# Moving the 32-bit conversion of the last weight from the expert stage to the gate and value products, with the first gate blocks spread out and the last rank product picked by name

## The chip, the cores and the metric

The kernel runs on one core of a Trainium2 chip. A core has TensorE (PE in the profile; its weight loads are PEld), VectorE (DVE), ScalarE (ACT), GpSimd (POOL) and SyncE (SP), which here only issues transfers. Each engine executes its own instructions in order and waits on semaphores for the others. The metric is the device time of one execution in microseconds (us).

## The reference, cut to what matters

Three parts follow one another. The weights of the third part are 64-bit floats in memory.

```
attn   = softmax(q k^T / 8 + bias from cumsum(s), causal) v      # 4 batches, 8 heads, 576 x 64
x      = attn as (2304, 512)                                     # one row for each token
logits = x @ w_gate + modality_bias[modality_id]                 # 8 experts
e      = argmax(logits);  g = softmax(logits)[e]
x      = g * (relu(x @ w1[e]) @ w2[e])                           # expert stage, 512 -> 1024 -> 512
out    = (sigmoid(x @ w_gate2) * (x @ w_val)) @ w_out            # 512 -> 1536 -> 512, float64 weights
```

## The kernel before, in words

**Stages.** Attention takes the 16 pairs of heads in a fixed order of operations (`PERIOD`). The expert stage follows: 9 slots of 256 tokens and 2 half slots of 128, each slot in 8 units, each unit 12 matmuls of the first product (`mm1`, L1004) and 12 of the second product of the unit before (`mm2`, L1024). The units are numbered u = 0 to 71; u = 0 to 15 serve slots 0 and 1 in turn. The gate and value stage (`Moe2.run`) has 36 units of 7 slots, each slot 6 matmuls (L1382) of one product in a fast-multiplication scheme; m = 0 is a gate unit, m = 1 a value unit. The output product ends the kernel (L1537, L1588). Almost every product is made of 3 matmuls over high and low parts, so ScalarE and VectorE split each operand into two.

**The router.** `Router.batch` appends the small operations of one batch to a queue: the logits with the bias as a ninth column (`lg`, copied on GpSimd at L642, summed at L644), maximum, one-hot `oh`, and then `ranks`, which counts with 6 small matmuls how many earlier tokens chose the same expert (`rp`, L656 and L658), then 5 indirect writes into a table on GpSimd's queue (L687). During attention `tick` takes one entry at a time from this queue; for batches 0 to 2 `ranks` waits (`hold`) for a place beside another product. The last batch is left over when attention ends, and `pump` takes entries after each unit u of the expert stage: 9 after u = 0, none after u = 1 and 2, 14 from u = 3 on. When the queue is empty the planning of the slots (`slots`, L782) is queued and pumped likewise; its result is the list of tokens of each slot (`tid`, transposed on TensorE as `itr`, L742, after u = 10).

**The conversion.** `Decode` turns a block of 64-bit floats into 32-bit floats in four tasks of successive steps: `near` on GpSimd (L877), `far` on VectorE (L881), `word` on ScalarE (L885), `tail` on VectorE (L890). SyncE loads the block (`load`, L866), and `tail` issues the next load. The gate and value weights go through it in blocks of 128 x 256, of which the first 8 are converted in the expert stage, one block for every two units from u = 45 on (four tasks each), and 40 in the gate and value stage. The last weight is converted in `last_weight` during the expert stage, in 12 blocks of 128 x 512, one for every two units from u = 17 on, and stored as 32-bit floats in memory (`wo32`); the output stage reads it back.

**The splitting of the gate and value weights.** After its 4 blocks are converted, each set of blocks is summed and split in 7 successive slots (`parts`: `high` on ScalarE L1353, `low` on VectorE L1356, `sub` on VectorE L1359). There are 10 such stretches in the gate and value stage; in 5 of them value units (m = 1) run, in 5 gate units. `snap` (L1391) copies bank X on ScalarE between two products that add to the same bank, so the next X product waits for it.

Of the kernel before, what the change touches and what calls it, by code (L numbers as in the profile page):

```python
# [8 lines left out]
F32 = mybir.dt.float32  # L9
# [491 lines left out]
TROWS, PUMPS = 96, (9, 0, 0, 14)  # L501
# [5 lines left out]
class Router:  # L507
# [92 lines left out]

    def apart(self, group, inst):

        inst = inst.ins
        self.tc.declare_no_dep(inst, group=group, reason="different rows")
        self.tc.add_to_no_dep_group(group, inst)
        self.apart_of[group].append(inst)
# [15 lines left out]
    def batch(self, b, xr, lg):  # L622
# [12 lines left out]
        tb = self.tb.rearrange("p (b t) e -> p b t e", t=5)[:, b]  # L635
# [6 lines left out]
        q.append(lambda: nc.gpsimd.tensor_copy(lg[:, :, :, 8], tb))  # L642
        self.space(4)
        q.append(lambda: V.tensor_reduce(L.unsqueeze(3), lg, axis=AX.X, op=ALU.add))  # L644
        q.append(lambda: V.tensor_reduce(mx.unsqueeze(2), L, axis=AX.X, op=ALU.max))
# [26 lines left out]
        q.append(lambda: V.tensor_tensor(L, L, bc(mx), ALU.subtract))  # L672
        q.append(ranks)
# [83 lines left out]
    def pump(self, n):  # L757
        self.q = [f for f in self.q if f]
        while self.q and n:
            self.q.pop(0)()  # L760
            n -= 1
# [86 lines left out]
class Decode:  # L848
# [7 lines left out]
    def __init__(self, tc, pool, n, srcs, bufs=2):  # L856
        self.nc, self.pool, self.srcs, self.size, self.bufs = tc.nc, pool, srcs, n, bufs
        self.raw, self.n, self.i = {}, 0, 0

    def load(self):  # L860

        if self.n < len(self.srcs):
            src = self.srcs[self.n]
            c, w = src.shape[1:]
            t = self.raw[self.n] = self.pool.tile([128, 8 * self.size], U8, tag="dr", name="dr", bufs=self.bufs)
            self.nc.sync.dma_start(t.rearrange("p (c b) -> p c b", c=c)[:, :, :w], src)  # L866
            self.n += 1

    def stages(self, dst, then=None):

        nc, V, o, i, n = self.nc, self.nc.vector, {}, self.i, self.size
        self.i += 1
        top = lambda: self.raw[i].bitcast(I8).rearrange("p (a b) -> p a b", b=8)[:, :, 4]

        def near():
            o["n"] = self.pool.tile([128, n], I8, tag="dn", name="dn", bufs=2)
            nc.gpsimd.tensor_scalar(o["n"], top(), 56.0, -56.0, ALU.min, ALU.max)  # L877

        def far():
            o["d"] = self.pool.tile([128, n], I8, tag="dd", name="dd", bufs=2)  # L880
            V.scalar_tensor_tensor(out=o["d"], in0=top(), scalar=-72.0, in1=o["n"], op0=ALU.max, op1=ALU.subtract)  # L881

        def word():
            o["t"] = dst()
            nc.scalar.activation(o["t"].bitcast(I32), o["d"], AF.Copy, scale=float(1 << 27))  # L885

        def tail():
            w = self.raw.pop(i).bitcast(I32).rearrange("p (a b) -> p a b", b=2)[:, :, 0]
            t = o["t"].bitcast(I32)
            V.scalar_tensor_tensor(out=t, in0=w, scalar=5, in1=t, op0=ALU.logical_shift_right, op1=ALU.bitwise_or)  # L890
            self.load()
            if then:
                then(o["t"])

        return [near, far, word, tail]
# [362 lines left out]
class Moe2:  # L1258
# [10 lines left out]
    def __init__(self, tc, moe, x2, ids2, wg, wv, wo, out, hd, keep, rp, wo32):  # L1269
# [8 lines left out]
        self.dec = Decode(tc, keep, 256, srcs)  # L1278
# [11 lines left out]
    def last_weight(self, pool):  # L1290

        dec = Decode(self.tc, pool, 512, [self.wo[128 * f : 128 * f + 128, 3:].rearrange("(c p) b -> p c b", c=1) for f in range(12)], 3)
        for _ in range(3):
            dec.load()
        new = lambda: pool.tile([128, 512], F32, tag="dt", name="dt", bufs=2)
        return [dec.stages(new, lambda t, f=f: self.nc.sync.dma_start(self.wo32[128 * f : 128 * f + 128, :], t)) for f in range(12)]
# [365 lines left out]
    def run(self, ctx, rest):  # L1662
# [26 lines left out]
        spread(at(12, 0), at(15, 0), self.rows())  # L1689
        free = 0  # L1690
# [48 lines left out]
        p = []  # L1739
# [24 lines left out]
def kernel(ctx, tc, q, k, v, s, modality_id, moe_w_gate, modality_bias, w1, w2, wg, wv, wo, out):  # L1764
# [10 lines left out]
    with tc.manual_schedule():  # L1775
        ident = cp.tile([128, 128], F32, name="ident")
        make_identity(nc, ident)
        ps_ctx, at_ctx, mo_ctx, ea_ctx, mw_ctx, ex_ctx, xs_ctx, wo_ctx, x1_ctx = (ExitStack() for _ in range(9))
# [44 lines left out]
        def main(u):  # L1823
            if u >= 0:
                router.pump(PUMPS[min(u, 3)])
# [113 lines left out]
```

## Time and profile before

| | |
|---|---|
| median of 3 runs | 933.51 us (931.78 to 933.62) |
| profiled execution, its own time | 931.2 us |
| span of its trace | 929.3 us |
| TensorE busy (matmuls) | 890.6 us, 96% of the span |
| VectorE, ScalarE, GpSimd busy | 687.5, 547.2, 395.8 us |
| mean granted TensorE clock | 0.992 of full speed |

The profiled execution's time is 1.9 us more than the span of its trace. Busy times of different engines overlap, so they do not add up; what bounds a stage has to be read from the stage.

### The profile page before, as it was taken

To read this page: it belongs to the slowest core of one execution; us is meant where nothing else is said; L and a number is where in the kernel's file an instruction comes from. 1 tells how busy PE (TensorE), PEld (TensorE's weight loads), DVE (VectorE), ACT (ScalarE), POOL (GpSimd) and SP (SyncE) were. 2 spreads that over 40 slices of the span, in tenths; PEclk is the share of its full clock that TensorE was granted. 3 is DMA by queue.
4 is the path that set the end of the run, shared out by engine and by line. 5 is a ranking of instruction groups with operands and counts; after the bars stand their busy time and mean duration, and the time that the engine had idled before them with its cause. 6 is when DMAs were issued, how large, how long until landed. Compare 5 with 4: busy or idle time off the path is not lost. (4 is left out here: it accounts for less than half of the span.)

```text
span 929.3 us, 18666 instructions
## 1 busy us (share of the span) xinstructions
PE 890.6 (96%) x6261; PEld 856.7 (92%) x6261; DVE 687.5 (74%) x1549; ACT 547.2 (59%) x1282; POOL 395.8 (43%) x626
## 2 busy tenths in 40 slices
PE   7999999999889998999999999999999999999996
PEld 6898899898789998999998999999999998889996
DVE  5899999999765688867667766767575747868770
ACT  5999899898633656666544545354535345454440
POOL 7988889898822676776620001010000000111111
PEclk8999999999999999999999999999999999999998
DMA  6667659676314458523566422424242308573501
GB/s 170 155 146 177 142 94 141 154 146 225 97 22 80 143 176 262 193 92 92 178 211 215 114 81 80 139 78 136 74 139 68 116 18 300 153 225 110 170 35 45
DMA packets 163866, 125.29 MB, mean 135 GB/s; under 512 B 86737, under 2 KB 147692, under 8 KB 163254
## 3 DMA queue, kind: packets, MB, share of 16 engines
q1 hardware_dynamic: 158566, 112.44, 43.2%
q0 software_dynamic: 3984, 11.32, 4.3%
q8 instruction: 50, 0.82, 0.4%
q14 instruction: 50, 0.41, 0.2%
q10 hardware_dynamic: 1216, 0.30, 0.1%
HBM read 115.95 MB, written 33.23 MB: 161 GB/s over the span
## 5 line engine op out<-in xcount | busy, mean ns | idle before, releaser
L1382 PE MATMUL X<-a,set 128*128 128x384 f32 x864 | 164.1, 337 | 1.9 <-ACT u L1391 0.9
L1382 PEld LDWEIGHTS X<-a,set 128*128 128x128 f32 x864 | 151.7, 188 | 3.8 <-ACT u L1391 1.9
L877 POOL TENSOR_SCALAR dn<-dr 128x256 int8<-128x256 int8 (+1 forms) x60 | 34.4, 573 | 249.0 <-DMA dr<-in_moe_w_val_dram 91.3
L940 POOL TENSOR_TENSOR w<-raw,w 128x512 fp32r<-128x512 f32 x56 | 80.3, 1444 | 45.9 <-ACT w L937 43.6
L1519 POOL DMA_INDIRECT out_dram<-oy,row x18 | 20.2, 1120 | 167.5 <-ACT oy L1543 91.4
L175 POOL TENSOR_SCALAR bias<-cumB,cumT 128x576 f32<-128x576 f32 (+4 forms) x155 | 82.9, 537 | 19.3 <-DVE nm L294 18.3
L1004 PE MATMUL ph<-xT,w 128*128 128x256 f32 x672 | 88.6, 280 | 0.0
L1004 PEld LDWEIGHTS ph<-xT,w 128*128 128x128 f32 x672 | 82.4, 188 | 0.0
L1382 PE MATMUL Y<-a,set 128*128 128x384 f32 x432 | 81.5, 336 | 0.0
L303 ACT ACTIVATE P<-P,nm 128x576 f32<-128x576 f32 (+3 forms) x128 | 79.6, 628 | 0.6 <-DVE nm L294 0.6
L338 DVE TENSOR_TENSOR PL<-pt,PH 128x512 fp32r<-128x512 f32 (+1 forms) x128 | 76.9, 630 | 3.1 <-ACT PH L331 2.6
L1382 PEld LDWEIGHTS Y<-a,set 128*128 128x128 f32 x432 | 76.0, 188 | 0.1
L294 DVE CUSTOM_DVE_ANT_0 P<-sb,bias 128x320 f32<-128x320 f32 (+3 forms) x128 | 67.3, 550 | 6.4 <-PE sb L285 4.8
L1391 ACT COPY u<-X 128x384 f32<-128x384 f32 x72 | 34.5, 480 | 61.1 <-PE X L1382 61.0
L331 ACT CAST PH<-pt 128x512 fp32r<-128x512 f32 (+1 forms) x128 | 64.7, 551 | 5.8 <-PE pt L322 4.7
L322 PE MATMUL pt<-ident,P 128*128 128x128 f32 x448 | 64.1, 277 | 2.8 <-DVE QL L241 1.0
L1008 ACT ACTIVATE hH<-ph 128x256 fp32r<-128x256 f32 x72 | 27.7, 384 | 62.3 <-PE ph L1004 56.4
L940 DVE TENSOR_TENSOR w<-raw,w 128x512 fp32r<-128x512 f32 x56 | 54.7, 976 | 12.1 <-ACT w L937 11.4
L937 ACT CAST w<-raw 128x512 fp32r<-128x512 f32 x112 | 63.6, 619 | 0.0
L285 PE MATMUL sb<-KT,QH 128*128 128x288 f32 (+3 forms) x192 | 56.6, 319 | 4.7 <-DVE nm L294 4.2
L322 PEld LDWEIGHTS pt<-ident,P 128*128 128x128 f32 x448 | 51.6, 142 | 7.8 <-ACT P L303 3.2
L1317 ACT CAST hf<-hp 128x768 fp32r<-128x768 f32 x42 | 34.1, 835 | 38.9 <-DVE hp L1319 35.2
(317 smaller groups left out, 2393.2 us busy)
## 6 DMA issues: line engine op xcount, KB each, us to landing
raw<-in_moe_w_dram SPq DMA_DIRECT2D x80, 512.0 KB
h<-sg SPq DMA_DIRECT2D x72, 192.0 KB
cumB<-cum_d SPq DMA_DIRECT2D x32, 288.0 KB
hp<-h SPq DMA_DIRECT2D x24, 384.0 KB
qraw<-in_q_dram SPq DMA_DIRECT2D x58, 128.0 KB
dr<-in_moe_w_out_dram SPq DMA_DIRECT2D x12, 511.6 KB
dr<-in_moe_w_gate_dram SPq DMA_DIRECT2D x24, 255.2 KB
dr<-in_moe_w_val_dram SPq DMA_DIRECT2D x24, 255.2 KB
```

Of the source, the lines that this page charges most:

```text
L175: (nc.vector if n in FILLB else nc.gpsimd).tensor_scalar(res[i][:rows], cumB[:rows, :m], -1.0, self.cumT[:rows, i, n : n + 1], ALU.mult, A ...
L285: nc.tensor.matmul(self.sb[:rows, o : o + c1 - c0], X[:, T0[i] : T0[i] + rows], h["KT"][:, c0:c1], start=j == 0, stop=j == 1)
L294: nc.vector.tensor_tensor_reduce(out=pt[:rows, :m], in0=self.sb[:rows, o : o + m], in1=self.bias_t[n][i][:rows], op0=ALU.add, op1=ALU.min, ...
L303: nc.scalar.activation(h["P"][i][:rows, : T0[i] + rows], h["P"][i][:rows, : T0[i] + rows], AF.Exp, bias=h["nm", i][:rows], scale=-1.0, acc ...
L322: nc.tensor.transpose(pt[:, c : c + 128], h["P"][i][:, T0[j] : T0[j] + 128], self.ident)
L331: self.nc.scalar.copy(t[:, :z], pt[:, :z])
L338: self.nc.vector.tensor_tensor(t[:, :z], pt[:, :z], h["H"][u][:, :z].bitcast(F32), ALU.subtract)
L937: nc.scalar.copy(v, src)
L940: (eng or nc.vector).tensor_tensor(v, src, h.bitcast(F32), ALU.subtract)
L1004: nc.tensor.matmul(ph, w[:, 128 * dc : 128 * dc + 128], x[:, dc], start=k == 0, stop=k == 11)
L1382: self.nc.tensor.matmul(bank, w[:, c], a[:, h, c], start=first and k == 0, stop=k == 5, skip_group_check=True)
L1391: self.nc.scalar.copy(t, self.o[u, "X"])
```

## The change

The last weight is converted during the gate and value stage, in 24 blocks of 128 x 256 instead of 12 of 128 x 512: block k has its four tasks at slots 31 + 26k/3 (rounded down) to 3 slots later, of 252 slots. The buffers are the space of an activation tile that is free then and of one weight tile. The first 8 gate blocks take one block for every four units from u = 24 on (loads of the first two at u = 23, before at u = 44). The bias copies are made one batch ahead, outside the queue's order of the batch. `pump` takes 14 entries whenever it takes any, but after u = 0 it stops in front of the last batch's `ranks`, so that `ranks` comes after u = 3.

```diff
-TROWS, PUMPS = 96, (9, 0, 0, 14)
+TROWS, PUMP, RANKS = 96, 14, 3
@@ mod_weights
+        for b in range(2):
+            self.bias_in(b)
+
+    def bias_in(self, b):
+        self.nc.gpsimd.tensor_copy(self.lg[b % 2][:, :, :, 8], self.tb.rearrange("p (b t) e -> p b t e", t=5)[:, b])
@@ batch
-        q.append(lambda: nc.gpsimd.tensor_copy(lg[:, :, :, 8], tb))
-        self.space(4)
         q.append(lambda: V.tensor_reduce(L.unsqueeze(3), lg, axis=AX.X, op=ALU.add))
+        if b + 2 < self.B:
+            q.append(lambda: self.bias_in(b + 2))
...
+        if b == self.B - 1:
+            self.last_ranks = ranks
         q.append(ranks)
@@ pump
-    def pump(self, n):
+    def pump(self, u):
         self.q = [f for f in self.q if f]
-        while self.q and n:
+        n = 0 if 0 < u < RANKS else PUMP
+        while self.q and n and (u or self.q[0] is not self.last_ranks):
@@ last_weight
-        dec = Decode(self.tc, pool, 512, [self.wo[128 * f : 128 * f + 128, 3:].rearrange("(c p) b -> p c b", c=1) for f in range(12)], 3)
-        for _ in range(3):
+        raw = [self.ap.tile([128, 3072], U8, tag=f"xs{i}", name=f"dx{i}", bufs=1) for i in range(3)]
+        top = self.rp.tile([128, 4096], U8, tag="raw2_3", name="dx3", bufs=1)
...
+        at = [(128 * f, 256 * l) for f in range(12) for l in range(2)]
+        dec = Decode(self.tc, 256, [
+            self.wo[r : r + 128, 8 * c + 3 : 8 * c + 2048].rearrange("(c p) b -> p c b", c=1) for r, c in at
+        ], room)
+        for _ in range(4):
             dec.load()
@@ Moe2.run
+        def last_weight():
+            for k, stages in enumerate(self.last_weight()):
+                for i, task in enumerate(stages):
+                    put(at(4, 3) + 26 * k // 3 + i, [task])
+
+        put(at(3, 5), [last_weight])
@@ kernel
-        for k, stages in enumerate(glu.last_weight(pool(wo_ctx, "dec", side="right", reuse_waits="tile"))):
-            for i, task in enumerate(stages):
-                put(2 * k + i - 55, [task])
-        put(-28, [wo_ctx.close, open_xs, glu.dec.load, glu.dec.load])
+        put(-49, [open_xs, glu.dec.load, glu.dec.load])
-                put(2 * k + i - 27, [task])
+                put(4 * k + i - 48, [task])
```

## Rows read from the trace of the kernel before

**Rows 1.** By stretch: us; busy (instructions) of PE, PEld, DVE, ACT, POOL; clock; DMA; GB/s.

```profile
309.00:390.00 81.00, 75.57 (x634) 73.85 (x633) 66.64 (x82) 50.61 (x104) 60.32 (x51) 1.00 0.65 211
...
390.00:460.00 70.00, 69.72 (x596) 69.52 (x595) 50.74 (x71) 42.17 (x92) 49.53 (x43) 1.00 0.33 101
...
545.00:757.00 212.00, 212.00 (x1212) 211.77 (x1212) 140.54 (x309) 99.61 (x222) 16.09 (x34) 1.00 0.29 95
```

**Rows 2.** TensorE's waits, by window: total us, times, longest.

```profile
PE rp L656 <- DVE oh L649: 4.5, 1, 4.5
...
PE sb L1024 <- DVE hL L1009: 3.4, 3, 1.5
PE y L1024 <- DVE hL L1009: 1.6, 3, 0.9
```

**Rows 3.** Timeline, end of attention: start, us, engine, line, output, count.

```profile
252.99 1.04 PE L988 MATMUL mtr<-ident,xg 128*128 128x128 f32 x8
...
255.56 1.29 DVE L994 TENSOR_TENSOR xT<-mtr,xT 128x512 fp32r<-128x512 f32 x2 [1.50 <-ACT xT L993]
...
258.50 0.20 PE L656 MATMUL rp<-oh,tri 128*128 128x48 bf16 x1 [4.48 <-DVE oh L649]
258.67 2.86 PE L1004 MATMUL ph<-xT,ew 128*128 128x256 f32 x12
...
263.12 1.60 PE L1004 MATMUL ph<-xT,ew 128*128 128x256 f32 x12
...
266.00 1.60 PE L1004 MATMUL ph<-xT,ew 128*128 128x256 f32 x12
```

**Rows 4.** By stretch, TensorE alone: us, busy (matmuls), granted clock, DMA, GB/s.

```profile
239.00:241.00 2.00, 0.51 (x5) 1.00 0.90 316
...
258.00:260.00 2.00, 1.50 (x12) 0.68 0.00 0
260.00:262.00 2.00, 2.00 (x12) 0.50 0.03 8
```

**Rows 5.** Timeline, from the ranks to the list of tokens.

```profile
268.40 0.19 DVE L677 TENSOR_TENSOR R<-R,oh 128x40 f32<-128x40 f32 x1
...
286.93 0.61 SPq L1047 DMA_DIRECT2D ids<-tid  x2
...
289.13 0.31 PE L742 MATMUL itr<-ident,tid 40*128 40x40 f32 x2
```

**Rows 6.** VectorE's groups, 309 to 391 us: count, busy us, mean ns, idle before.

```profile
L890 DVE SCALAR_TENSOR_TENSOR dt<-dr,dt 128x512 int32<-128x512 int32 x12 | 17.6, 1469 | 0.0
L881 DVE SCALAR_TENSOR_TENSOR dd<-dr,dn 128x512 int8<-128x512 int8 x12 | 15.7, 1311 | 2.6 <-POOL dn L877 2.6
```

**Rows 7.** VectorE's and GpSimd's groups, 545 to 757 us.

```profile
L1412 DVE TENSOR_TENSOR sg<-u,sg 128x384 f32<-128x384 f32 x28 | 15.9, 567 | 1.0
...
L890 DVE SCALAR_TENSOR_TENSOR ds<-dr,ds 128x256 int32<-128x256 int32 x36 | 14.7, 419 | 3.3 <-ACT ds L885 2.9
L881 DVE SCALAR_TENSOR_TENSOR dd<-dr,dn 128x256 int8<-128x256 int8 x36 | 14.1, 422 | 0.3 <-POOL dn L877 0.3
...
L877 POOL TENSOR_SCALAR dn<-dr 128x256 int8<-128x256 int8 x34 | 16.1, 473 | 175.6 <-DMA dr<-in_moe_w_val_dram 80.9 <-DMA dr<-in_moe_w_gate_dram 44.6 <-DVE sg L1403 29.6
```

**Rows 8.** Timeline of ScalarE in two stretches of weight splitting among value units.

```profile
636.47 0.47 ACT L1391 COPY u<-X 128x384 f32<-128x384 f32 x1
...
680.39 0.47 ACT L1391 COPY u<-X 128x384 f32<-128x384 f32 x1
```

**Rows 9.** Chain that ended last: TensorE's pieces behind those copies.

```profile
637.14 2.21 PE X L1382 x12
...
681.26 2.08 PE X L1382 x12
```

**Rows 10.** Timeline, first batch of the router during attention.

```profile
108.30 0.23 DVE L672 TENSOR_TENSOR r_L<-r_L,r_mx 128x40 f32<-128x40 f32 x1
...
112.05 0.19 PE L656 MATMUL ptx<-oh,tri 128*128 128x48 bf16 x1
```

More of the change, by code (lines that the diff above doesn't have):

```diff
@@ L634, in batch @@
         bc = lambda a: a.unsqueeze(2).to_broadcast([128, 5, 8])
-        tb = self.tb.rearrange("p (b t) e -> p b t e", t=5)[:, b]
         L, mx, eq, em = (tile_([128, 5, 8], "L"), tile_([128, 5], "mx"), tile_([128, 5, 8], "eq"), tile_([128, 5], "em"))
@@ L848, with __init__, pool_room @@
 class Decode:
-    def __init__(self, tc, pool, n, srcs, bufs=2):
-        self.nc, self.pool, self.srcs, self.size, self.bufs = tc.nc, pool, srcs, n, bufs
+    def __init__(self, tc, n, srcs, room):
+        self.nc, self.room, self.srcs, self.size = tc.nc, room, srcs, n
         self.raw, self.n, self.i = {}, 0, 0
+    @staticmethod
+    def pool_room(pool, n):
+        shapes = {"dr": ([128, 8 * n], U8), "dn": ([128, n], I8), "dd": ([128, n], I8)}
+        return lambda tag, i: pool.tile(*shapes[tag], tag=tag, name=tag, bufs=2)
     def load(self):
@@ L864, in load @@
             c, w = src.shape[1:]
-            t = self.raw[self.n] = self.pool.tile([128, 8 * self.size], U8, tag="dr", name="dr", bufs=self.bufs)
+            t = self.raw[self.n] = self.room("dr", self.n)
             self.nc.sync.dma_start(t.rearrange("p (c b) -> p c b", c=c)[:, :, :w], src)
@@ L869, in stages @@
     def stages(self, dst, then=None):
-        nc, V, o, i, n = self.nc, self.nc.vector, {}, self.i, self.size
+        nc, V, o, i = self.nc, self.nc.vector, {}, self.i
         self.i += 1
@@ L875, in near @@
         def near():
-            o["n"] = self.pool.tile([128, n], I8, tag="dn", name="dn", bufs=2)
+            o["n"] = self.room("dn", i)
             nc.gpsimd.tensor_scalar(o["n"], top(), 56.0, -56.0, ALU.min, ALU.max)
         def far():
-            o["d"] = self.pool.tile([128, n], I8, tag="dd", name="dd", bufs=2)
+            o["d"] = self.room("dd", i)
             V.scalar_tensor_tensor(out=o["d"], in0=top(), scalar=-72.0, in1=o["n"], op0=ALU.max, op1=ALU.subtract)
@@ L1277, in __init__ @@
         srcs = [cols(w, f, j, l).rearrange("(c p) b -> p c b", p=128) for f in range(self.NF) for w in (wg, wv) for j, l in blocks]
-        self.dec = Decode(tc, keep, 256, srcs)
+        self.dec = Decode(tc, 256, srcs, Decode.pool_room(keep, 256))
         self.wo = wo.bitcast(U8)
@@ L1286, in preload, with last_weight @@
         self.nc.scalar.activation(t, t, AF.Sigmoid)
-    def last_weight(self, pool):
-        dec = Decode(self.tc, pool, 512, [self.wo[128 * f : 128 * f + 128, 3:].rearrange("(c p) b -> p c b", c=1) for f in range(12)], 3)
-        for _ in range(3):
+    def last_weight(self):
+        raw = [self.ap.tile([128, 3072], U8, tag=f"xs{i}", name=f"dx{i}", bufs=1) for i in range(3)]
+        top = self.rp.tile([128, 4096], U8, tag="raw2_3", name="dx3", bufs=1)
+        dr = [raw[0][:, 0:2048], raw[1][:, 0:2048], top[:, 0:2048], top[:, 2048:4096]]
+        cut = lambda a, n, k: raw[2][:, a + n * k : a + n * k + n]
+        places = {
+            "dr": dr, "dn": [cut(0, 256, k).bitcast(I8) for k in range(2)],
+            "dd": [cut(512, 256, k).bitcast(I8) for k in range(2)], "dt": [cut(1024, 1024, k).bitcast(F32) for k in range(2)],
+        }
+        room = lambda tag, i: places[tag][i % len(places[tag])]
+        at = [(128 * f, 256 * l) for f in range(12) for l in range(2)]
[3 more added lines that the diff above has]
+        for _ in range(4):
             dec.load()
-        new = lambda: pool.tile([128, 512], F32, tag="dt", name="dt", bufs=2)
-        return [dec.stages(new, lambda t, f=f: self.nc.sync.dma_start(self.wo32[128 * f : 128 * f + 128, :], t)) for f in range(12)]
+        store = lambda t, r, c: self.nc.sync.dma_start(self.wo32[r : r + 128, c : c + 256], t)
+        return [dec.stages(lambda k=k: room("dt", k), lambda t, r=r, c=c: store(t, r, c)) for k, (r, c) in enumerate(at)]
     def load_x(self, t, raws):
@@ L1777 @@
         make_identity(nc, ident)
-        ps_ctx, at_ctx, mo_ctx, ea_ctx, mw_ctx, ex_ctx, xs_ctx, wo_ctx, x1_ctx = (ExitStack() for _ in range(9))
+        ps_ctx, at_ctx, mo_ctx, ea_ctx, mw_ctx, ex_ctx, xs_ctx, x1_ctx = (ExitStack() for _ in range(8))
         ps = pool(ps_ctx, "psum", space=PSUM)
@@ L1824, in main @@
             if u >= 0:
-                router.pump(PUMPS[min(u, 3)])
+                router.pump(u)
             if not router.q and phase[0] == 0:
```

## Prediction

> **What bounds the kernel now.** I read the busy times by stretch first, then TensorE's waits window by window, then the timeline where a wait stands. The reader is to see that TensorE sets the time almost everywhere, so that only its gaps can be won and only new gaps can cost. In the gate and value stage it is busy for all of 212 us, while VectorE is busy for 140.5 us of them and GpSimd for 16.1 [rows 1]. In the expert stage two stretches differ: from 309 to 390 us, where the last weight is converted, TensorE is busy for 75.57 of 81 us; from 390 to 460 us, where gate blocks are converted instead, for 69.72 of 70 [rows 1]. VectorE's share falls between them from 66.64/81 = 82% to 50.74/70 = 72%. TensorE's waits in the first of them are for `hL`, which VectorE makes: 3.4 + 1.6 = 5.0 us [rows 2]. The other large wait is a single one, 4.5 us for `oh` in front of the last rank product [rows 2], at the end of attention.
>
> **The change part by part.**
>
> *The last rank product.* After the transposes of slot 1 (252.99 + 1.04 = 254.03) TensorE's next instruction is `rp` at 258.50, which waits for the router's chain on VectorE; only then comes the first product of unit 1, at 258.67 [rows 3]. With `rp` after u = 3, that product waits for its own operand `xT` alone: VectorE makes it in two halves, 255.56 to 256.85 [rows 3], so the first half is there at 255.56 + 1.29/2 = 256.2, and the second at 256.85, before the seventh of the 12 matmuls wants it. A unit at full clock takes 266.00 - 263.12 = 2.88 us [rows 3]. Unit 2 would begin at 256.2 + 2.88 = 259.1 instead of 263.12, which is 4.0 us earlier. The six small matmuls still have to run later, 258.67 - 258.50 = 0.17 us, and a little around them, so I take 3.7.
>
> In this sum 1.6 us are clock: behind the wait of 4.48 us the granted clock is 0.68, then 0.50, which is 1.2 GHz, and the unit from 258.67 to 263.12 takes 4.45 us instead of 2.88 [rows 3, 4]. Would the clock fall again behind the gap that is left, 256.2 - 254.03 = 2.2 us? Between 239 and 241 us TensorE is busy for only 0.51 of 2 us and the clock stays at 1.00 [rows 4]. The new gap is nearer to that one than to 4.48, so I take no fall; with a fall the gain is 4.0 - 1.6 - 0.2 = 2.2. The bounds of this term are 2.2 and 4.0.
>
> What is queued behind the moved product: the ranks, the table writes, the list of tokens, its transposes `itr`. Before, the multiplication with the ranks began at 268.40, right behind `hL` of unit 3 [rows 5]. It will now wait until TensorE has ended unit 3's second product (1.44 us, half a unit), the rank product and its addition, about 1 us later against TensorE. The list had arrived by 286.93 and `itr` ran at 289.13 [rows 5], so some 2.2 us of slack are there, and 1.2 stay. If that cover were gone, each microsecond over it would come back on TensorE.
>
> *The bias copies and the four removed empty entries.* Four copies on GpSimd of about 0.27 us move, and the chain of a batch starts some entries earlier. In the first batch that chain ended at 108.30, but its rank product had to wait for its place at 112.05 [rows 10], as it will again: nothing behind the hold moves. I take 0; bounds are 4 x 0.27 = 1.1 us either way, if VectorE's order around them or GpSimd's wait for the sum were felt.
>
> *What leaves the expert stage.* Twelve blocks take VectorE 12 x (1.469 + 1.311) = 33.4 us, half of its 66.64 us in that stretch [rows 1, 6], plus ScalarE, GpSimd and transfers. The gain has two readings. By idle time: 81 - 75.57 = 5.43 us, less what stays at the later stretch's rate, 0.28 x 75/70 = 0.3, gives 5.1. By counts: 634 matmuls in 81 us against 596 in 70; at the later rate they take 634 x 70/596 = 74.5 us, which gives 6.5 [rows 1]. The second also holds what is lost when the matmuls around a stall run further apart, so I lean to it: 6.0. The eight gate blocks come into this stretch at half their old density; at the old one TensorE lost 0.28 us in 70 [rows 1], so they cost nothing. SyncE's queue loses twelve loads and twelve stores among the expert weights, for which TensorE does not wait now; nothing is gained there.
>
> *What comes into the gate and value stage.* One block is 0.473 us on GpSimd, 0.422 + 0.419 us on VectorE and one word on ScalarE [rows 7]: for 24 blocks 24 x 0.841 = 20.2 us of VectorE, which has 212 - 140.5 = 71.5 us free [rows 1]. The same four tasks run there 36 times now without a wait of TensorE. What hides them is slack, and it is thin in one kind of place: the stretches in which weights are split while value units run. There ScalarE's `high` waits for VectorE's `sub`, the snap queues behind it, and the next X product needs the snap. The snap ends at 636.94 and the product starts at 637.14; the next time 680.86 and 681.26 [rows 8, 9]: slack of 0.2 and 0.4 us. By the slots of the new blocks, `tail` falls in front of that `sub` in two of these five stretches and `far` in two others, 0.42 us each; so each may add up to about 0.4 less its slack. In the fifth the block follows it. I take 0.8 us for all five and for the ScalarE-heavy stretches of gate units, with bounds 0 and 5 x 0.84 = 4.2. SyncE waits with each new load and store for the `tail` before it; behind it stand stores of products, read much later, and the loads of gate and value blocks, for which GpSimd already waits [rows 7] while TensorE does not. The stores end at slot 234, the reading back starts at slot 243.
>
> GpSimd's `near` runs among VectorE's work: `sg<-u,sg` took 567 ns on average with 34 of them in the window, little over its sibling forms [rows 7]. The Trainium skill, page "SBUF — State Buffer", section "Who interferes with whom", says that a VectorE instruction with two SBUF inputs and a GpSimd instruction that reads SBUF exclude each other for the whole instruction. By that rule one more 0.473 us would be lost in each of the five tight stretches, 2.4 us, and the stage would cost 3.2 instead of 0.8; the trace so far bears little of it out.
>
> *The sum.* 931.2 - 3.7 - 6.0 + 0.8 = 922.3 us for an execution like the profiled one. The median of the runs is 2.3 us above it, so 924.6 us, a gain of 8.9 us or 1.0%.
>
> **The rivals.** *A: the clock falls all the same, or the first product of unit 1 finds another wait.* Rank gain 2.2 or less: 926.1. For it: the clock's reaction to a gap of 2.2 us is not in the trace, and `hL` of unit 1 comes behind the chain and a weight split on VectorE, about 0.3 us ahead of its use. Against it: rows of 4.
>
> *B: the gate and value stage gives part of it back.* VectorE's lag reaches the snaps in most of the ten stretches, or the exclusion above holds: 3 to 6 us, so 927 to 930. For it: slacks of 0.2 and 0.4 us. Against: 36 blocks without a wait.
>
> *C: the waits of the expert stage stay.* If VectorE and GpSimd are late for the splitting of the expert weights and not for the conversion, the gain there is 0 to 2 us, and the time 929 to 931. Against it: the next stretch has the same splitting, 0.28 us idle.
>
> *D: slower.* VectorE sets the pace of the gate and value stage. If each of its new instructions delays TensorE in full, 20.2 us come in: 933.5 - 9.7 + 20.2 = 944.0. It decides from 9.7/24 = 0.40 us a block on, one of the two instructions. For it: VectorE runs without a gap in the splitting stretches. Against it: 71.5 us free, and between those stretches it waits for TensorE.
>
> **How the numbers follow.** Forecast 0.64, A 0.14, B 0.13, C 0.04, D 0.05. The predicted time is the forecast's, 924.6. Its lower end: gains of 4.0 and 6.5, no cost, 933.5 - 10.5 = 923.0, and 2 us for the spread of the runs (931.78 to 933.62) and the bias term: 921. The upper end takes in A and most of B: 930. About 0.2% of the time, 1.9 us, is what a measurement of this kernel can tell from no change. Faster by more than that needs under 931.6: forecast, A, nearly all of B, half of C, 0.91; within it 0.04; slower 0.05.
>
> **What would show it.** Right: `rp` in the trace after unit 3 without a wait, a gap in front of unit 1's first product of about 2.2 us with the clock at 1.00 behind it; between units 17 and 41 some 8.5 matmuls a us, as from 390 to 460 us [rows 1], with TensorE idle under 0.5 us; in the gate and value stage 2.1 to 2.2 us for 12 matmuls throughout [rows 9]. Wrong: new waits of X products for `u` on ScalarE above 2 us in total, waits for `hL` that stay, `itr` waiting for the list, or a clock of 0.50 after attention.

## The result, and the profile after

The changed kernel takes 920.75 us (median of 5 runs, 920.44 to 922.45) where the kernel before took 933.62 us beside it: a ratio of 0.9866, 95% interval 0.985 to 0.9882, or 12.5 us by the ratio. The forecast was 924.6 us with 921 to 930 around it: faster, as said, and 0.25 us under the lower end. The profiled execution after takes 920.75 us, with a span of 918.5 us (before 929.3), so the spans differ by 10.8 us.

By stretch, as in [rows 1] (us; busy and instructions of PE, PEld, DVE, ACT, POOL; clock; DMA; GB/s), the kernel after:

```profile
309.00:390.00 81.00, 81.00 (x694) 81.00 (x693) 44.54 (x76) 49.13 (x105) 57.62 (x48) 1.00 0.38 121
390.00:460.00 70.00, 70.00 (x598) 70.00 (x597) 37.48 (x60) 40.56 (x85) 45.22 (x36) 1.00 0.39 125
545.00:757.00 212.00, 210.52 (x1200) 209.21 (x1199) 153.83 (x345) 105.21 (x241) 27.22 (x56) 1.00 0.40 132
```

In the first stretch TensorE has no idle time any more, and 694 matmuls stand where 634 stood. In the third it has 1.48 us of it, where there was none.

TensorE's waits from 245 to 500 us and from 545 to 770 us (total us, times, longest), answering [rows 2]:

```profile
PE yh L1135 <- DVE hT L1126: 2.7, 3, 1.3
PE ph L1017 <- ACT xT L1006: 2.4, 1, 2.4
...
PE ph L1017 <- DVE xT L1007: 0.3, 1, 0.3
...
PE X L1407 <- ACT u L1416: 1.5, 3, 0.9
```

The waits for `oh` and for `hL` are gone. The wait for `hT`, at the end of the expert stage, was there before with 3.4 us. New are a wait of the first product of unit 1 for `xT`, and three waits of X products for the copies of ScalarE.

The end of attention, TensorE's timeline (start, us, then engine, line, output, count), as [rows 3]:

```profile
250.64 1.04 PE L1001 MATMUL mtr<-ident,xg 128*128 128x128 f32 x8
254.07 0.39 PE L1017 MATMUL ph<-xT,ew 128*128 128x256 f32 x1 [2.40 <-ACT xT L1006]
254.80 1.58 PE L1017 MATMUL ph<-xT,ew 128*128 128x256 f32 x11 [0.34 <-DVE xT L1007]
257.66 1.60 PE L1017 MATMUL ph<-xT,ew 128*128 128x256 f32 x12
...
263.41 0.20 PE L661 MATMUL rp<-oh,tri 128*128 128x48 bf16 x1
...
263.58 1.68 PE L1017 MATMUL ph<-xT,ew 128*128 128x256 f32 x12
```

The rank product `rp` stands behind unit 3 and waits for nothing. Unit 1 takes 257.66 - 254.07 = 3.59 us, where it took 4.45 us [rows 3]. The granted clock is 1.00 in every 2 us from 252 to 264 us; before it fell to 0.50 [rows 4].

The list of tokens, as [rows 5]:

```profile
264.00 0.20 DVE L684 TENSOR_TENSOR R<-R,oh 128x40 f32<-128x40 f32 x1
...
283.91 0.31 PE L749 MATMUL itr<-ident,tid 40*128 40x40 f32 x2
...
284.13 0.62 SPq L1060 DMA_DIRECT2D ids<-tid  x2
```

In the first batch the router's chain ends 2.7 us earlier than in [rows 10]; its rank product still waits for its place, which comes 0.9 us earlier:

```profile
105.58 0.64 DVE L677 TENSOR_TENSOR r_L<-r_L,r_mx 128x40 f32<-128x40 f32 x1
...
111.16 0.19 PE L661 MATMUL ptx<-oh,tri 128*128 128x48 bf16 x1
```

In the gate and value stage (groups from 545 to 757 us, as [rows 7]: count, busy us, mean ns, idle before), the new blocks are the `dx` rows, close to the prices that the forecast used, and `sg<-u,sg` beside them takes 558 ns (before 567). The 12 large blocks of [rows 6] are gone from the expert stage.

```profile
L1437 DVE TENSOR_TENSOR sg<-u,sg 128x384 f32<-128x384 f32 x27 | 15.1, 558 | 0.9
L894 DVE SCALAR_TENSOR_TENSOR dx<-dx,dx 128x256 int8<-128x256 int8 x23 | 10.0, 436 | 0.0
L903 DVE SCALAR_TENSOR_TENSOR dx<-dx,dx 128x256 int32<-128x256 int32 x23 | 9.6, 418 | 2.0 <-ACT dx L898 2.0
...
L890 POOL TENSOR_SCALAR dx<-dx 128x256 int8<-128x256 int8 x22 | 10.6, 489 | 3.8 <-DVE dx L894 3.8
```

Between the first and the last Z product of this stage there are 260.02 us, 2.46 us more than before. Set beside each other unit by unit, five steps make the loss: 0.3, 1.1, 0.3, 0.3 and 0.7 us, at units 5, 7, 16, 22 and 28, each in a stretch in which weights are split. The largest is seen in the timeline (SPq is SyncE's queue):

```profile
547.36 0.33 SPq L879 DMA_DIRECT2D dx<-in_moe_w_out_dram  x1
547.74 0.42 SPq L1320 DMA_DIRECT2D wo<-dx  x1
548.22 0.42 SPq L1438 DMA_DIRECT2D h<-sg  x1
...
548.75 0.94 SPq L879 DMA_DIRECT2D dr<-in_moe_w_val_dram  x2
...
554.02 0.40 POOL L890 TENSOR_SCALAR dn<-dr 128x256 int8<-128x256 int8 x1 [19.21 <-DMA dr<-in_moe_w_val_dram]
554.46 0.43 DVE L894 SCALAR_TENSOR_TENSOR dd<-dr,dn 128x256 int8<-128x256 int8 x1 [1.75 <-POOL dn L890]
...
558.27 0.47 ACT L1416 COPY u<-X 128x384 f32<-128x384 f32 x1
...
558.79 2.34 PE L1407 MATMUL X<-a,set 128*128 128x384 f32 x12 [0.87 <-ACT u L1416]
```

A load and a store of a new block, both behind that block's `tail`, go out ahead of the loads of two value blocks. Those land for GpSimd's `dn` at 554.02, 5.3 us after their issue; VectorE's `dd` waits for it, the split that follows is late, ScalarE's snap too, and the X product waits 0.87 us.

At two of the other steps, the snap of ScalarE and the chain's piece behind it, as [rows 8, 9]:

```profile
624.80 0.47 ACT L1416 COPY u<-X 128x384 f32<-128x384 f32 x1
...
669.06 0.47 ACT L1416 COPY u<-X 128x384 f32<-128x384 f32 x1
```

```profile
625.33 2.34 PE X L1407 x12
632.87 2.10 PE X L1407 x12
...
669.59 2.35 PE X L1407 x12
```

The snap ends at 625.27, the product starts at 625.33, and such a piece takes 2.34 us where its neighbours take 2.10. The slack there was thinner than [rows 9] make it look: in the chain a piece starts where the one before it ends, and the timeline of the kernel before has the product of 637.14 at 637.00, 0.06 us behind the snap, with its weights already waiting for the snap:

```profile
637.00 2.03 PEld L1382 LDWEIGHTS X<-a,set 128*128 128x128 f32 x12 [0.18 <-ACT u L1391]
637.00 2.34 PE L1382 MATMUL X<-a,set 128*128 128x384 f32 x12
```

The span's 10.8 us lie so, from milestones of both timelines: attention (to `mtr` of slot 1) 2.35; from there to unit 5, 2.87; units 17 to 41, 7.22; units 42 to 70, 0.19; unit 71 to the first Z, 0.47; Z to Z -2.46; the rest 0.16.

### The profile page after: what moved, and what is told of

It is laid out like the page before. It is cut to its first block, busy times and chain, and to the rows that moved or that the text cites. A ratio compares the mean times of both kernels' runs of the same rounds, so it can differ in the third digit from the quotient of the medians.

```text
span 918.5 us, 18756 instructions
## 1 busy us (share of the span) xinstructions
PE 888.4 (97%) x6261; PEld 853.9 (93%) x6261; DVE 667.2 (73%) x1573; ACT 547.2 (60%) x1294; POOL 397.2 (43%) x638
## 5 line engine op out<-in xcount | busy, mean ns | idle before, releaser
L890 POOL TENSOR_SCALAR dn<-dr 128x256 int8<-128x256 int8 x48 | 24.5, 512 | 227.5 <-DMA dr<-in_moe_w_val_dram 95.7
L1022 DVE SCALAR_TENSOR_TENSOR hL<-ph,hH 128x256 fp32r<-128x256 f32 x72 | 30.4, 422 | 49.2 <-ACT hH L1021 47.6
L953 DVE TENSOR_TENSOR w<-raw,w 128x512 fp32r<-128x512 f32 x56 | 46.6, 832 | 19.2 <-ACT w L950 18.0
```

The lines of the kernel that those rows point to most:

```text
L953: (eng or nc.vector).tensor_tensor(v, src, h.bitcast(F32), ALU.subtract)
```

## The experiments

Microseconds gained are by the ratio to the kernel before, run on the same chip beside it, times 930, its median there (929.57, 930.43 and 930.00 us in the three groups of runs).

**The three parts alone.** `e1_rank_only`, the kernel before with

```diff
-        while self.q and n:
+        n = 0 if 0 < u < RANKS else PUMP
+        while self.q and n and (u or self.q[0] is not self.last_ranks):
```

> The kernel before with the last rank product moved behind unit 3 and nothing else; biases and conversion stay as they were. My theory: the move by itself is worth what its place in the trace says, 2.9 to 3.7 us, so about 3.0 us under the kernel before, with the clock at 1.00 where it was 0.50, no wait for oh, and the transposes of slot 1 at the end of attention at their old time, within 0.3 us. Rival: the 2.35 us by which attention itself ended earlier in the changed kernel come from the order of the router's work, which the move touches too; then this kernel ends attention 1 to 2.4 us earlier as well and is 4 to 6 us faster.

927.01 us, ratio 0.9975 (0.9958 to 0.9993): 2.3 us gained. There is no wait for `oh`, the clock stays at 1.00, and attention ends at 252.62 us, within 0.4 us of before. The theory holds, its size within the interval.

`e2_bias_only`, the kernel before with the copies taken out of the batches' chains and the queue's counts shortened by one:

```diff
+        for b in range(2):
+            self.bias_in(b)
...
-        q.append(lambda: nc.gpsimd.tensor_copy(lg[:, :, :, 8], tb))
-        self.space(4)
```

> The kernel before with only the bias copies taken out of the batches' chains and the four empty entries removed; the last rank product stays before unit 1. The prediction gave this part 0 with 1.1 us either way. Theory: this part is what made attention end 2.35 us earlier in the changed kernel, because each batch's chain is shorter by one GpSimd copy and four empty entries; then the transposes of slot 1 come 1.5 to 2.4 us earlier here and the time falls by 1.5 to 2.5 us, while the wait for oh of about 4.5 us and the clock of 0.50 behind it stay. Rival: those 2.35 us are variation from one profiled execution to the next; then attention ends within 0.5 us of the kernel before and the time is within 1 us of it.

929.92 us, ratio 1.0002 (0.9986 to 1.0019). The profiled execution ends attention at 249.68 us, 3.3 us before the first profile of the kernel before, and its time is 927.49 us, yet the median is the same. The theory's place was right in one profile and its time wrong over 12 runs.

`e3_weight_late`, the kernel before with the other half of the change:

```diff
-        for k, stages in enumerate(glu.last_weight(pool(wo_ctx, "dec", side="right", reuse_waits="tile"))):
...
+                    put(at(4, 3) + 26 * k // 3 + i, [task])
...
-                put(2 * k + i - 27, [task])
+                put(4 * k + i - 48, [task])
```

> The kernel before with only the conversion moved: the last weight in 24 blocks during the gate and value stage, the first gate blocks in every fourth unit; biases and the last rank product as before. Theory: units 17 to 41 take about 70.5 us instead of 77.9 and the expert stage gains 7.4 us in all, the gate and value stage gives 2.45 us back, so 4.9 us net, about 928.6 us, with attention and the wait for oh as before. Rival: part of the 7.4 us came from the units starting earlier and at full clock, not from the conversion; then the stage gains under 6 us and the net is under 3.5 us.

925.68 us, ratio 0.9958 (0.9942 to 0.9973): 3.9 us gained. Units 17 to 41 take 72.89 us from first product to first product (before 80.11), and the five steps stand at the same units with 0.33, 1.23, 0.35, 0.27 and 0.68 us, 2.71 us from Z to Z. So they belong to the blocks alone. The stages say 4.9 us, inside the interval.

**The parts in pairs, and both kernels again.** The parts alone add up to 6.0 us (2.3 - 0.2 + 3.9), the changed kernel had 12.5. So the pairs were run: `e9_rank_weight` (the changed kernel with the biases as before), `e10_bias_weight` (with the last rank product before unit 1) and `e11_rank_bias` (with the conversion in the expert stage), and once more the changed kernel (`e7_after_again`) and the kernel before (`e8_before_again`), neither edited. The edit of `e10_bias_weight`:

```diff
-        n = 0 if 0 < u < RANKS else PUMP
-        while self.q and n and (u or self.q[0] is not self.last_ranks):
+        n = (8, 0, 0, 14)[min(u, 3)]
+        while self.q and n:
```

`e9_rank_weight` undoes the edit of `e2_bias_only`, `e11_rank_bias` that of `e3_weight_late`.

> The changed kernel once more, beside the kernel before, on the chip of the next runs. The rank move alone gave 2.3 us and the conversion alone 3.9 us, the biases nothing: 6.2 us where the changed kernel had 12.9 us in its first comparison. Theory: the parts add up, by the stages of the traces 3.1 to 3.7 + 7.5 - 2.4 = 8.2 to 8.8 us, and the rest of the first comparison is a matter of which runs of the kernel before it met, so the gain here is 8 to 9 us and attention's end differs by up to 3 us between profiled executions of the same code. Rival: the parts help one another, and the gain stays at 11.5 us or more.

> The kernel before, profiled a second time. In its first profile unit 5 began 18.77 us after the transposes of slot 1, in the two kernels with the same order there 17.45 us, and the wait for oh was 4.48 us against 3.17 us. Theory: that 1.3 us is a chance of the first profiled execution, as is the time at which attention ends: here 17.4 to 17.5 us and a wait for oh of 3.1 to 3.2 us. Rival: the two other kernels shortened it; then 18.7 us and 4.5 us again. In either case units 17 to 71 take 165.1 to 165.8 us.

> The changed kernel with the bias copies as in the kernel before: rank move and conversion together. The changed kernel gave 10.2 us beside the parts' 2.5, 0 and 3.9. Theory: the stages add up, as in the traces (rank 2.7, conversion and thinner gate blocks 7.1 + 0.5, gate and value stage -2.5), and single comparisons are off by 1 to 2 us; then about 8 us under the kernel before, with unit 5 at 266.0 us as in the other kernels with the later rank product. Rival one: the bias copies give 2 to 3 us as soon as the rank product is out of the way; then only 6.4 us. Rival two: rank move and conversion help one another; then 10 us.

> The changed kernel with the last rank product before unit 1 again. Theory: stages add up, 7.1 + 0.5 - 2.5 = 5.1 us under the kernel before; the wait for oh is 3.17 us, and unit 5 begins at 267.1 to 269.4 us, depending on attention's end and on whether the clock falls behind that wait. Rival: the bias copies count with the conversion; then 7 us or more.

> The changed kernel with the conversion in the expert stage as before, rank move and bias copies together. Theory: 2.7 us under the kernel before, as the rank move alone (2.5 us measured); units 17 to 42 take 79.5 to 80.1 us. Rival: the bias copies give 2 to 3 us once the rank product is out of the way; then 5 us under the kernel before, and unit 5 begins before 265 us.

| part moved | median, us | ratio (95%) | gained, us |
|---|---|---|---|
| rank | 927.01 | 0.9975 (0.9958 to 0.9993) | 2.3 |
| bias | 929.92 | 1.0002 (0.9986 to 1.0019) | -0.2 |
| weight | 925.68 | 0.9958 (0.9942 to 0.9973) | 3.9 |
| rank, weight | 922.05 | 0.9901 (0.9872 to 0.993) | 9.2 |
| bias, weight | 923.68 | 0.9923 (0.9896 to 0.9951) | 7.2 |
| rank, bias | 925.91 | 0.9947 (0.9929 to 0.9965) | 4.9 |
| all three | 920.22 | 0.989 (0.9871 to 0.9908) | 10.2 |

Each part can be read four times, as the difference that it makes with each choice of the others. Weight: 3.9, 9.2 - 2.3 = 6.9, 7.2 + 0.2 = 7.4, 10.2 - 4.9 = 5.3; mean 5.9. Rank: 2.3, 5.3, 5.1, 3.0; mean 3.9. Bias: -0.2, 2.6, 3.3, 1.0; mean 1.7. A single ratio is good for some 2 us either way, so a mean over four such pairs for about 1.4 (worked out as 2 x the root of 8, over 4), and no reading stands out from its mean by more than two ratios can differ. Neither rival with parts that help one another is shown; the kernels with one part alone came out low, all three. Against their expectations: the changed kernel's 10.2 us lie between theory and rival. The two pairs with the bias copies gained what their rivals said (7.2 and 4.9 us, theories 5.1 and 2.7), and unit 5 begins at 264.22 us in the pair of rank and bias, before 265; the pair without the copies gained 9.2, between its theory's 8 and the 10 of its second rival.

What the profiles show of it, with the times from `mtr` of slot 1 to unit 5, and from unit 17 to unit 42:

| profile | end of attention | wait for `oh` | to unit 5 | 17 to 42 |
|---|---|---|---|---|
| before | 252.99 | 4.48 | 18.77 | 80.11 |
| before again | 251.42 | 3.17 | 15.97 | 80.09 |
| bias | 249.68 | 3.16 | 17.46 | 79.54 |
| weight | 251.75 | 3.17 | 17.44 | 72.89 |
| bias, weight | 252.98 | 3.16 | 17.46 | 72.89 |
| rank | 252.62 | none | 13.75 | 79.90 |
| rank, bias | 250.48 | none | 13.74 | 80.30 |
| rank, weight | 256.96 | none | 13.75 | 72.89 |
| after | 250.64 | none | 15.90 | 72.89 |
| after again | 252.58 | none | 13.75 | 72.89 |

The conversion's 6.7 to 7.4 us are as steady as a number can be. The rank product's are 3.7 us (17.45 - 13.75) or 2.2 us (15.97 - 13.75), and the difference is the clock. Behind the same wait of 3.17 us the kernel with only the weight moved fell to half the clock and the second profile of the kernel before did not (2 us each, TensorE alone: busy, matmuls, clock, DMA, GB/s; first the kernel with the weight moved, then the kernel before again):

```profile
254.00:256.00 2.00, 0.05 (x2) 1.00 0.01 0
256.00:258.00 2.00, 2.00 (x18) 0.72 0.00 0
258.00:260.00 2.00, 2.00 (x11) 0.50 0.12 8
```

```profile
254.00:256.00 2.00, 0.37 (x8) 1.00 0.00 0
256.00:258.00 2.00, 2.00 (x18) 1.00 0.12 8
258.00:260.00 2.00, 2.00 (x19) 1.00 0.00 0
```

So my expectation of 17.4 to 17.5 us for the kernel before again was wrong by the clock, and right on the wait. Both first profiles have something that no later one has: ScalarE's `xT` starts 1.95 us (before) and 2.80 us (after) behind the start of `mtr`, in the 12 others 0.64 us. That is the 1.31 us by which the first wait for `oh` was longer, and the 2.16 us by which the first profile after was slower to unit 5. What held ScalarE there is open.

Attention ends on average at 251.7 us in the nine profiles with the copies ahead and at 253.2 us in the five without (256.96 among them), with a scatter of 2 to 3 us in each, so the ends alone don't price the copies. A stretch that repeats does. From the start of the sixth group of `ot` products in attention to that of the twelfth (69.52 to 113.67 us before, 69.38 to 112.78 after), four of the five profiles without take 44.10 to 44.19 us and all nine with them 43.38 to 43.48: 0.75 us. Of this 0.47 us stand at one place (first the kernel before, then after):

```profile
77.23 0.51 PE L361 MATMUL ot<-PH,vhl 128*128 128x512 f32 x1 [1.02 <-DVE QL L259]
```

```profile
76.06 0.41 POOL L605 COPY lg<-tb 128x40 f32<-128x40 f32 x2 [4.79 <-DVE tb L599]
76.66 0.50 PE L361 MATMUL ot<-PH,vhl 128*128 128x512 f32 x1 [0.55 <-DVE QL L259]
```

The copies of the first two batches now stand in GpSimd's order right behind the making of `tb`, the table of biases, and GpSimd is idle until it is there. VectorE's five instructions that make it take 1.30 to 1.31 us in all beside the idle GpSimd, in each of the nine profiles, and 1.75 to 1.77 us beside a busy one in four of the other five. The fifth is the 256.96 (rank and weight moved): there they take 3.62 us, the last of them alone 1.45 beside a GpSimd instruction, where it takes 0.33 in the others.

```profile
75.67 1.40 POOL L203 TENSOR_TENSOR khl<-kraw,khl 128x576 fp32r<-128x576 f32 x1
75.79 1.45 DVE L599 TENSOR_TENSOR tb<-tb,fill 128x160 f32<-128x160 f32 x1
```

TensorE then waits 3.25 us for `QL`, the clock falls behind the wait, and the stretch takes 47.95 us. What the copies give beyond the 0.75 us, within the 1.7 and its 1.4 either way, stays open.

The clock adds to the scatter of the ends. Behind the gap that [rows 4] show, 1.26 to 1.60 us long at 237 to 243 us, it stayed at 1.00 in eight of the 14 profiles and fell in six, which cost some 1.5 us each (2 us each, TensorE alone; first after, then `e12_placed_two`, an experiment below):

```profile
240.00:242.00 2.00, 2.00 (x13) 1.00 0.03 4
```

```profile
240.00:242.00 2.00, 1.94 (x9) 0.59 0.03 4
```

In the profile after, the list's transposes `itr` no longer have slack. In the second profile of the changed kernel they waited:

```profile
284.41 0.31 PE L749 MATMUL itr<-ident,tid 40*128 40x40 f32 x2 [0.64 <-DMA tid<-tab,row]
```

In the kernel with rank and weight moved the wait is 0.77 us, in one other kernel 0.3 us, in the rest none.

**The loss of the gate and value stage.** `e4_no_conversion`, the changed kernel whose new blocks only load and store, so that the conversion itself is left out:

```diff
-        return [dec.stages(lambda k=k: room("dt", k), lambda t, r=r, c=c: store(t, r, c)) for k, (r, c) in enumerate(at)]
+        zero = places["dt"][0]
+        self.nc.vector.memset(zero, 0.0)
+        return [[lambda: None] * 3 + [lambda r=r, c=c: (dec.load(), store(zero, r, c))] for r, c in at]
```

> The changed kernel without the four engine instructions of each of the 24 blocks: their loads and stores stay in their queue, the stores write zeros, so the last product has a zero weight. Theory: of the 2.45 us that the gate and value stage gave back, some 1.1 us at unit 7 come from loads of value blocks that stand behind a load and a store of the new blocks in SyncE's queue. In the changed kernel that queue waits there for VectorE's tail; without the tail it doesn't wait, so that here nearly all 2.45 us come back and the time is about 918.3 us. Rival one: it is the bytes of the new transfers, not the wait, that delay those loads; then the 1.1 us at unit 7 stay and the time is about 919.4 us. Rival two: the stage's loss isn't the blocks' at all; then the time stays at 920.7 us.

919.33 us, ratio 0.9882 (0.9858 to 0.9906). All five steps are gone, that of unit 7 too. The value blocks' loads are issued at 547.20 us instead of 548.75, and `dn` begins 2.9 us behind them instead of 5.3:

```profile
544.30 0.42 SPq L879 DMA_DIRECT2D dx<-in_moe_w_out_dram  x1
544.77 0.44 SPq L1320 DMA_DIRECT2D wo<-dx  x1
...
547.20 1.38 SPq L879 DMA_DIRECT2D dr<-in_moe_w_val_dram  x2
...
550.12 0.58 POOL L890 TENSOR_SCALAR dn<-dr 128x256 int8<-128x256 int8 x1 [19.47 <-DMA dr<-in_moe_w_val_dram]
```

The same bytes pass here, so it is not the bytes (rival one) but when they pass: behind a `tail` that VectorE is late with, and just ahead of loads that are needed. The first of those loads also needs its own block's `tail`, which VectorE starts at 547.68 us after and at 546.72 here: 0.96 of the 1.55 us are VectorE's, the rest is the queue's. The median alone is what rival one gave, 919.4, and over the theory's 918.3; it is the steps in the trace that decide between them. From Z to Z 1.05 us remain, spread over the units without a wait behind 545 us; the kernel with the bias part alone, which has no new block there, shows 0.78 us of the same drift. What makes it is open.

`e5_placed` and `e12_placed_two` keep the work and move the blocks' slots:

```diff
+PLACE = (37, 45, 50, 55, 64, 75, 83, 88, 93, 102, 106, 122, 128, 134, 143, 148, 164, 170, 176, 185, 190, 206, 213, 220)
...
-                    put(at(4, 3) + 26 * k // 3 + i, [task])
+                    put(PLACE[k] + i, [task])
```

The second has 73, 82, 91, 95 in place of 75, 83, 88, 93.

> The changed kernel with the 24 blocks at other slots: no far, word or tail of a block stands in front of a sub of a value stretch, and no tail comes just before a load of a value block. Theory: the five steps of 0.3, 1.1, 0.3, 0.3 and 0.7 us come from those places alone (without the engine instructions they were gone, the late loads too); then the gate and value stage loses under 0.5 us against the kernel before instead of 2.46, and the time is about 2 us under the changed kernel's on this chip. Rival: each block in a busy stretch costs the same wherever it stands, because VectorE and GpSimd share their way to SBUF; then other steps take the place of the five, 1.5 us or more in all, and the time is within 1 us of the changed kernel's.

> The changed kernel with the blocks at the other slots, and four of them moved once more, out of the stretch of units 13 and 14, where the first placing met a weight split of a gate block and gave 1.04 us back. Theory: that step goes and none takes its place, so the first to the last Z take 258.2 to 258.6 us, and the time is 1 us under the first placing's 918.9, about 12 us under the kernel before. Rival: the moved blocks meet another split; then the stage stays at 259.3 us or more.

`e5_placed`: 918.89 us, ratio 0.9868 (0.9846 to 0.9889); beside it the changed kernel had 920.22. The five steps are gone, but a new one of 1.08 us stands at units 13 and 14, where a block's `word` and `tail` met the split of a gate block, and a drift of some 0.6 us follows it: 1.71 us in all, so the theory's 0.5 was missed. `e12_placed_two`: 917.48 us, ratio 0.9854 (0.9826 to 0.9882), the fastest kernel here by median. From Z to Z it takes 257.71 us, 0.15 us more than before and less than its theory's 258.2, with all 24 blocks in place (a step of 0.33 us is left at unit 14, half of it won back behind it):

```profile
545.00:757.00 212.00, 211.93 (x1212) 211.61 (x1212) 154.78 (x347) 105.25 (x241) 26.68 (x56) 1.00 0.43 137
```

VectorE does in this window what it does in the changed kernel (154.78 against 153.83 us), and TensorE's idle time is 0.07 instead of 1.48 us. So the loss is one of place, all but 0.15 us of it. Between the two versions and the changed kernel the times differ by 1.3 and 2.7 us and their ratios' intervals overlap; the steps in the traces do not.

**The thinner gate blocks.** `e6_gate_dense`:

```diff
-        put(-49, [open_xs, glu.dec.load, glu.dec.load])
+        put(-28, [open_xs, glu.dec.load, glu.dec.load])
...
-                put(4 * k + i - 48, [task])
+                put(2 * k + i - 27, [task])
```

> The changed kernel with the first gate blocks at the kernel before's density and place, every second unit from unit 45 on. The prediction costed the thinner spacing at nothing. Theory: units 17 to 41 are empty of conversion then and take 70.5 us as now, the later units 70.5 to 70.7 us as in the kernel before, so the time is within 0.5 us of the changed kernel's. Rival: with expert weights being split as well, four more tasks for every second unit make VectorE late by the 3.1 us that it lost in the conversion stretch of the kernel before, and the time is 2 to 4 us longer.

922.53 us, ratio 0.9915 (0.9896 to 0.9933), 2.3 us over the changed kernel beside it, with overlapping intervals. Units 17 to 41 take 72.89 us as before, units 42 to 70 take 85.71 us instead of 84.98. Of the two the trace's 0.7 us is what this edit shows; it lies between theory and rival. The five profiles of kernels with the conversion in the expert stage, which have the gate blocks at that density too, show 85.17 to 85.90 us there, all with the thinner blocks 84.98.

## Why the prediction came out as it did

**The base.** The forecast was a gain of 8.9 us under a median of 933.5. The changed kernel took 920.75 and 920.22 us in two groups of runs; the kernel before took 933.6 us in the first and 929.6 to 930.4 in the three later ones. Against those the gain is 10.2 us (ratio 0.989), 1.3 us more than forecast, where the first comparison makes it 3.6. The 2.3 us that the forecast added for "the median" of the kernel before did not apply: after's median is its profiled time. Without them the sum was 922.3, 1.5 us off. That it came so near is in part luck, for the errors of the parts nearly cancel: the expert stage gave 1.4 us more than taken, the copies 0.75 or more, the gate and value stage 1.7 less.

**The last rank product: right in kind, its size in part by luck.** Taken as 3.7; the profiles with the wait of 3.17 us show 3.7 where the clock had fallen and 2.2 where it had not, the four readings of the medians 3.9 in the mean. But the sum was 4.48 us of wait less a gap of 2.2 us that would be left, and both held the late `xT` of the first profiles: in the later ones the wait is 3.17 us, and the gap 0.24 us before the first matmul and 0.34 us before the next. The two errors nearly cancel. Between the two first profiles, where the gap was 2.40 us, the gain is 18.77 - 15.90 = 2.9 us. No fall of the clock came behind the new gap, but the reason given was not good: the gap of [rows 4], taken as one behind which the clock stays, is the one behind which it fell in six of 14 profiles. That `rp` and its six matmuls are cheap held. The step that failed in it is the cover: "some 2.2 us of slack are there, and 1.2 stay". `itr` waits 0.64 us in one of two profiles of the changed kernel, one of the forecast's own signs of being wrong, so the slack is used up.

**The bias copies: taken as nothing, worth 0.75 us or more.** "I take 0; bounds are 4 x 0.27 = 1.1 us either way." The medians give 1.7 with about 1.4 either way, the stretch of attention that repeats 0.75. The step that failed is "nothing behind the hold moves": the place of the first batch's rank product itself comes earlier, 111.16 us where it was 112.05 [rows 10], because time is won ahead of the hold. GpSimd's idle time while it waits for the table is what frees VectorE there.

**The expert stage: right in kind, 6.0 against 7.4.** Units 17 to 41 gain 7.2 us and the later ones 0.2. The reading by counts was the better one, and still low, in part because its yardstick, the stretch from 390 to 460 us, held gate blocks at their old density: at that stretch's rate after, 598 matmuls in 70 us, the 634 take 74.2 us, which gives 6.8 instead of 6.5, and at the first stretch's own, 694 in 81 us, 7.0. That the gate blocks cost nothing at half their density came true (72.89 us for units 17 to 41 with them and, in `e6_gate_dense`, without). The premise, "at the old one TensorE lost 0.28 us in 70", held for the one profile it was read from, with 0.2 us lost over units 42 to 70; in `e6_gate_dense` it is 0.7 us, in the four other profiles with that density 0.5 to 0.9. So thinning the blocks out is a gain that the forecast left out. Idle time understated the first stretch: 5.4 us idle, 7.2 us lost.

**The gate and value stage: wrong in size, 0.8 against 2.46.** The four stretches that the forecast named by their slots are places where a step stands, at 0.3, 0.3, 0.3 and 0.7 us instead of up to 0.4 less the slack, and the fifth has none, as said. The slack of 0.2 and 0.4 us was misread from [rows 9]; at the first place 0.06 us stood there. The chain `sub`, `high`, snap, X product is what the trace shows. One step was not foreseen, the 1.1 us at unit 7: "behind it stand stores of products, read much later, and the loads of gate and value blocks, for which GpSimd already waits [rows 7] while TensorE does not". GpSimd's wait was read as slack; it was the end of a chain whose next link, VectorE's `dd`, had none.

The Trainium skill, page "SBUF — State Buffer", section "Who interferes with whom", would have had a VectorE instruction with two SBUF inputs and a GpSimd instruction that reads SBUF exclude each other; by the forecast's estimate from it the stage would cost 3.2 us. The stage's total came near it, but the largest step, the 1.1 us at unit 7, is a late transfer. The trace agrees with the rule in kind, on single instructions: from the first to the last Z of the kernel after, 11 `dd<-dr,dn` overlap a GpSimd instruction and take 0.55 us in the mean, up to 0.65, where the others take 0.42, while `sg<-Y,u`, which reads a bank, keeps 0.56 beside one.

```profile
555.12 0.95 POOL L890 TENSOR_SCALAR dx<-dx 128x256 int8<-128x256 int8 x2
555.18 0.62 DVE L894 SCALAR_TENSOR_TENSOR dd<-dr,dn 128x256 int8<-128x256 int8 x1 [0.30 <-POOL dn L890]
```

It does not agree on the price. All VectorE instructions of the stage that read no bank and overlap one of GpSimd's take, over what their form takes alone, 1.2 us more in sum before, 3.8 after and 4.0 in `e12_placed_two`, and that kernel's stage loses 0.15 us. What part it has in the five steps is not separated. The mean of `sg<-u,sg` (558 ns after, 567 before [rows 7]) could not show it, because few of them meet a GpSimd instruction.

**The rivals.** A's other wait came, 2.40 us for `xT` in the first profile after, without a fall of the clock; its rank gain of 2.2 us is what comes out against the second profile of the kernel before, in which the clock did not fall. B gives 3 to 6 us back in the stage; 2.46 in the first profile after, 3.27 in the second, drift included, are at its edge, and its first cause, VectorE's lag reaching the snaps, is the one that was seen. C and D fall: no wait for `hL` is left, and 24 blocks cost 0.1 us each, not 0.40.

## What to carry to other kernels

Work moved into slack is paid by place, not by amount: the same 24 blocks cost 2.5 us or 0.15 us by the slots they had. So look for the stretches in which a chain over three engines ends just before TensorE needs it, and keep new work, and new entries of the transfer queue ahead of such a chain's loads, out of them. An engine that waits long for a transfer proves no slack behind it; ask what its successor waits for. And a yardstick taken from another stretch of the same trace carries that stretch's own losses. Where two profiles differ, compare stretches that repeat from one profile to the next, and not the times at which they begin.

## What the runs showed of the hardware that was not expected

Behind a gap of the same 3.17 us the granted clock fell to 0.50, the lower of its two levels, in three kernels (1.5 us lost), and stayed at 1.00 in one; behind the gap of 1.26 to 1.60 us near 240 us it fell in six profiles and stayed at 1.00 in eight. A gap's length alone did not decide it here.

A GpSimd instruction can lengthen VectorE's beside it: `tb<-tb,fill` took 1.45 us beside GpSimd's `khl` in one profile and 0.33 in 13, and `dd<-dr,dn` up to 0.65 instead of 0.42. In attention this reached TensorE (waits for `QL` of 1.02 and 3.25 us instead of 0.55), in the gate and value stage with well chosen slots hardly.

Two profiles of the kernel before reach unit 5 at 271.76 and 267.39 us, 4.4 us apart. From there to unit 17 all kernels without a wait of `itr` take 35.76 to 36.03 us, and from 17 to 42 nine profiles of eight kernels take 72.89 or 72.90 us. The kernels that wait for VectorE in that stretch scatter from 79.54 to 80.30. So a difference of 2 us at attention's end says nothing in a single profile, and one of 0.2 us in a stretch without waits does.
